# Earlier key and value loads with own buffers in a fused attention and mixture-of-experts kernel

## The chip, the cores and the metric

The kernel runs on one core of a Trainium2 chip. The metric is the device time of one execution in microseconds (us); the time before is the median of three runs.

## The reference

Three layers follow one another, all in float32: attention with a bias that a small network makes of relative positions, a token and channel mixer, and a mixture of experts in which each token goes to one expert. The change is in the attention:

```
B, H, S, D = q.shape                      # 2, 8, 576, 64
scores = np.matmul(q, k.transpose(0, 1, 3, 2)) / np.sqrt(D)
x = (log1p(abs(i - j)) / log1p(maximum(i, 1)))[..., None]
bias = np.maximum(x @ w1 + b1, 0.0) @ w2  # S x S x H, the same for both batches
attn = softmax(scores + bias.transpose(2, 0, 1))
out = np.matmul(attn, v)
```

## The kernel before

The order of all work is written out by hand. After a start section the attention runs in 40 steps. A step `s` stands for one tile of query rows, one batch and one pair of heads. The first tile holds the last 64 rows of the sequence for one pair (`it == NIT`); its eight steps, 0 to 7, take batch 0 in steps 0 to 3 and batch 1 in steps 4 to 7, two heads each. Then come four tiles of 128 rows with eight steps each, so step 8 is the first of tile 0. The mixers and the experts follow.

Keys: `load_k(i)` (L210) fetches the keys of four heads from HBM with five transfers, four of 128 KB (L216) and one of 64 KB (L217), in pieces of 256 bytes, into a buffer `kn`. There are two such buffers in turn: `load_k(0)` and `load_k(4)` share one, `load_k(2)` and `load_k(6)` the other. `key_T` (L251) transposes the keys on TensorE, ScalarE copies them into tiles `K` (L193), and `key_split` (L272) makes their low parts on VectorE. `key_T` and `key_split` of pair `s + 2` stand in step `s`.

Values: `load_v(b)` (L221) fetches all values of a batch with ten transfers, eight of 128 KB (L230) and two of 64 KB (L231), after two memsets on GpSimd (L228). `values` (L416) reads them first in step 2 for batch 0 and in step 6 for batch 1.

Bias: for each group of 16 rows `bias_hidden` (L478) makes the hidden layer on VectorE, ScalarE and GpSimd (L490, L487), `bias_mm` (L492) multiplies it with the second weights into PSUM, ScalarE copies that out into `ev` (L503), and a transfer brings `ev` into its rows of the bias tile: two transfers of 144 KB for each group of the last tile (L509, tile `bias4`), one of 288 KB for each group of the other tiles (L511). There are two `ev` buffers. The four groups of the last tile and the first of tile 0 stand in the start section, the other seven of tile 0 in steps 0 to 6. `softmax_tile` (L336) adds scores and bias and takes the maximum on VectorE (L337, a custom operation with output `t`) and the exponential on ScalarE (L340). It needs the whole bias tile: step 0 waits for all groups of `bias4`, step 8 for all eight of tile 0.

Queries: `load_q` (L234) loads queries into two buffers `qn`. The call in step 4 (L245) takes a buffer that `tail_split` of step 5 (L294, on GpSimd: L193 and L295 with output `qm`) must have read. Tiles from step 8 on have their split queries moved by four transfers of 128 KB each (L328, `qt<-qs`).

All these transfers are issued on one queue, that of SyncE (SP), in the order of the code: a transfer that has to wait holds all behind it. Eight semaphores serve them in turn, and an issue waits until the transfer eight places before it has landed. The order of the start section stands in the list `ORDER["start"]` (L58), the later loads in the loop over the steps (L659 to L662):

```
if s == 1:
    load_k(6)
if s == 2:
    load_v(1)
```

Of the kernel before, what the change touches and what calls it, by code (L numbers as in the profile page):

```python
# [9 lines left out]
F32 = mybir.dt.float32  # L10
# [11 lines left out]
B, H, S, D = 2, 8, 576, 64  # L22
# [32 lines left out]
QO = 3, 3, 3, 6  # L55

ORDER = {
    "start": "hidden0 const load_k2 tail_split0 hidden1 bias0 hidden2 bias1 key_T00 hidden3 zero key_T01 key_T11 key_T10 key_split0 tail_split1 bias2 hidden4 bias3 load_k4 hidden5 key_split1 tail_T bias4 load_v load_q".split(),  # L58
    "first": "scores0 hidden2 last_T prob_T0 values key_T0 normalize query_T tail_T query_split hidden1 hidden0 key_T1 bias_mm key_split out_T tail_split hidden3 query_rest".split(),
    "mixed": "hidden2 scores0 values tail_T query_T normalize hidden0 last_T prob_T0 key_T0 key_T1 query_split tail_split hidden1 key_split query_rest bias_mm out_T hidden3".split(),  # L60
    "bias": "query_T query_split hidden3 scores0 scores1 last_T values hidden0 query_rest hidden2 late bias_mm out_T mix prob_T0 prob_T1 hidden1 normalize".split(),
# [37 lines left out]
def body(ctx, tc, q, k, v, w1, b1, w2, wt1, wt2, wc1, wc2, wg, wl, mw1, mw2,  # L99
# [17 lines left out]
    with tc.manual_schedule():  # L117
        tok = ctx.enter_context(ExitStack())
        mix = TokenMix(nc, x)
        attention(tc, nc, tok, mix, q, k, v, w1, b1, w2, c_L, c_id, ident, x, wt1, wt2, prefill)  # L120
        if "x" in dbg:
            nc.sync.dma_start(dbg["x"], x)
        R = Routing(tc, nc, wg, wl, ident, c_tok, c_small, x2d, meta)
        X = Experts(tc, nc, R, Rings(tc, ctx, "big", side="right"), x_p, mw1, mw2, ident, x2d, meta, out)
        mixer(tc, nc, tok, mix, wc1, wc2, ident, x, R, X)
        if "x2" in dbg:
            nc.sync.dma_start(dbg["x2"], x2d)
        X.rest()
        X.close()
        R.close()  # L130


def attention(tc, nc, tok, mix, q, k, v, w1, b1, w2, c_L, c_id, ident, x, wt1, wt2, prefill):
# [9 lines left out]
    tw_p = pool(tok, "tokw")  # L143
    with ExitStack() as ctx:
        cst = pool(ctx, "acst")
        bias_p = pool(ctx, "bias", 2)
        nat_p = pool(ctx, "nat")
# [15 lines left out]
        def load_const():  # L163
            four = lambda ap, n: ap.rearrange("(a k) o -> a k o", a=1).to_broadcast([4, HID, n])

            cut = 4 * NG + S + 128
            warm = cst.tile([128, 1], F32, name="warm")
            nc.vector.memset(warm, 0.0)
            nc.scalar.activation(warm, warm, AF.Exp)
            nc.sync.dma_start(tabs[:, 0:cut], c_L[:, 0:cut])  # L170
            nc.scalar.dma_start(w1c, four(w1.rearrange("o k -> k o"), 1))
            nc.sync.dma_start(b1c, four(b1.rearrange("(k o) -> k o", o=1), 1))
            nc.sync.dma_start(w2r, four(w2, H))
            load_k(0)
            load_q(*steps[0])
            nc.sync.dma_start(tabs[:, cut:], c_L[:, cut:])
            nc.sync.dma_start(ident, c_id)

            zero = x[:, 0]
            nc.vector.memset(zero, 0.0)  # L180
            ps = alloc_ps()
            for _ in range(WARM):
                nc.tensor.matmul(ps, lhsT=zero[:, 0:128], rhs=zero, start=True, stop=True)
            nc.gpsimd.memset(wblk, 0.0)
            for ii in range(4):
                r = slice(32 * ii, 32 * ii + 32)
                nc.gpsimd.tensor_copy(wblk[r, 8 * ii:8 * ii + 8], w2r[r])
# [18 lines left out]


        nat = {}

        def load_k(i):  # L210

            b, pr = divmod(i, NP)
            n = nat_p.tile([128, 20, D], F32, name="kn", tag="kn", bufs=2)
            main, hs = n[:, 0:16].rearrange("p (n h) d -> p n h d", h=4), k[b, 2 * pr:2 * pr + 4]
            for j in range(NIT):
                nc.sync.dma_start(main[:, j], hs[:, 128 * j:128 * j + 128].rearrange("h p d -> p h d"))  # L216
            nc.sync.dma_start(n[0:64, 16:20], hs[:, 512:S].rearrange("h p d -> p h d"))  # L217
            for j in range(2):
                nat["k", i + j] = main[:, :, 2 * j:2 * j + 2], n[0:64, 16 + 2 * j:18 + 2 * j]

        def load_v(b):  # L221
            n = kv_p.tile([128, NIT + 1, H, D], F32, name=f"v{b}")


            nv, src = n.rearrange("p n (a e) d -> e p n a d", e=2), v[b].rearrange("(a e) p d -> e p a d", e=2)
            for e in range(2):
                r, z = (slice(64 * o, 64 * o + 64) for o in (e, 1 - e))
                nc.gpsimd.memset(nv[e][z, NIT], 0.0)  # L228
                for j in range(NIT):
                    nc.sync.dma_start(nv[e][:, j], src[e][64 * e + 128 * j:64 * e + 128 * j + 128])  # L230
                nc.sync.dma_start(nv[e][r, NIT], src[e][0:64] if e else src[e][512:S])  # L231
            nat["v", b] = n

        def load_q(it, i):  # L234

            b, pr = divmod(i, NP)
            n = nat_p.tile([128, 4, D], F32, name="qn", tag="qn", bufs=2)
            if it == NIT:
                tv = q[b, :, 512:S].rearrange("(a e) p d -> e p a d", e=2)
                for e in range(2):  # L240
                    nc.sync.dma_start(n[64 * e:64 * e + 64], tv[e])
                for j in range(NP):
                    nat["q", it, i + j] = n[:, j]
            else:
                nc.sync.dma_start(n, q[b, 2 * pr:2 * pr + 4, 128 * it:128 * it + 128].rearrange("h p d -> p h d"))  # L245
                nat["q", it, i] = n
# [271 lines left out]
        def fetch(p):  # L518
            n = p[1]
            if p[0] == 0:  # L520
                src = wt1[128 * n:min(128 * n + 128, S)]
            else:
                src = wt2[128 * n:128 * n + 128, HALF * p[2]:HALF * p[2] + HALF]
            raws[p] = fetch_f64(nc, nat_p, src, "kn", 2, p[0] == 0 and n == 4)
# [83 lines left out]
        def late_fetch(s):  # L608

            if pieces and any(f is decode for f, *_ in late.get(s, ())):  # L610
                fetch(pieces.pop(0))

        load_const()
        bias_setup()
        start = {
            "const": (bias_const,), "zero": (query_zero,), "load_k2": (load_k, 2), "load_k4": (load_k, 4), "load_v": (load_v, 0),
            "load_q": (load_q, *steps[NP]), "tail_T": (tail_T, *steps[0]),
        }
        for n in range(2):
# [11 lines left out]
        for s in range(N + 2):  # L631

            bias = gi < len(groups) and s < N and s >= B * NP * (its.index(groups[gi] // 8) - 1)
            at = lambda d, n=N: steps[s + d] if 0 <= s + d < n else None
            two = lambda d: (s + d) % 2 == 0 and s + d >= B * NP and at(d)
            hide = groups[gi + 1] if bias and gi + 1 < len(groups) else None
            todo = {
                "late": (late_step, (s,)), "mix": (mixes[s][0], mixes[s][1:]) if s in mixes else (None, None),
                "tail_split": (tail_split, at(2, B * NP)), "tail_T": (tail_T, at(1, B * NP)),
                "query_T": (query_T, two(QO[0])), "query_split": (query_split, two(QO[1])), "query_rest": (query_rest, two(QO[2])),  # L640
                "key_split": (key_split, at(2, B * NP)),
                "normalize": (normalize, at(0)), "last_T": (last_T, at(-1)),
                "values": (values, at(-2)), "out_T": (out_T, at(-2)),
                "bias_mm": (bias_mm, (groups[gi],) if bias else None),
            }
            for j in range(4):
                todo[f"hidden{j}"] = bias_hidden, hide is not None and (hide, (j,))
                todo[f"key_T{j}"] = key_T, j < 2 and at(2, B * NP) and (*at(2), j)
                todo[f"scores{j}"] = scores, at(0) and (*at(0), j)
                todo[f"prob_T{j}"] = prob_T, at(-1) and (*at(-1), j)  # L650
            if two(QO[3]):
                load_q(*steps[s + QO[3]])
            for name in ORDER["edge" if bias and s % (B * NP) == B * NP - 1 else "first" if s < 3 else "mixed" if s < B * NP else "bias" if bias else "plain"]:
                f, a = todo[name]
                if a:
                    f(*(a[1:] if f in (key_split, key_T) else a))
            gi += bias
            late_fetch(s - 1)
            if s == 1:  # L659
                load_k(6)  # L660
            if s == 2:
                load_v(1)  # L662
            if s == 10:
                prefill()
            if s == 8:
                for _ in range(2):
                    fetch(pieces.pop(0))
# [1095 lines left out]
```

## Time and profile before

| what | us |
|---|---|
| runs before | 583.7, 582.85, 583.69; median 583.69 |
| profiled execution | 584.03 |
| its span (first to last instruction) | 582.3 |
| PE busy in the span | 545.5 (94%) |
| DVE busy in the span | 383.9 (66%) |

The profiled execution takes 1.7 us more than its span, and 0.34 us more than the median. All times below are us from the start of the span. Engines: PE is TensorE, PEld its weight loads, DVE VectorE, ACT ScalarE, POOL GpSimd, SP SyncE; SPq is SyncE issuing a transfer, a name with `<-` is output and input of an instruction. An issue's duration is not that of the transfer. A wait in square brackets is the idle time of that engine just before the instruction, with what ended it.

### The profile page before, as it was taken

How to read it: one execution, taken by the hardware profiler on the slowest of the kernel's cores; microseconds unless marked ns; L12 is line 12 of the kernel's file. 1: busy time of each engine (PE TensorE's matmuls, PEld its weight loads, DVE VectorE, ACT ScalarE, POOL GpSimd, SP SyncE). 2: the span in 40 equal slices, each digit the busy share in tenths (PEclk: the TensorE clock that was granted, in tenths of full speed). 3: DMA queues.
4: the chain of work that ended last, by engine and by line, in shares of the span. 5: the costliest groups of instructions: out<-in, count | busy, mean ns of one | idle time of the engine just before them, and what ended most of it. 6: DMA issues, size and time to landing. Idle time of an engine off the chain costs nothing.

```text
span 582.3 us, 11959 instructions
## 1 busy us (share of the span) xinstructions
PE 545.5 (94%) x4306; PEld 430.3 (74%) x4306; DVE 383.9 (66%) x896; ACT 329.5 (57%) x608; POOL 242.1 (42%) x230
## 2 busy tenths in 40 slices
PE   7689699999899999989999999999999999999992
PEld 3366477777677887869999877787778778787871
DVE  5789588889887675698888535714473235668650
ACT  4678589789898793344444223221423257777760
POOL 4666547476555360044444300310014234657541
PEclk8979889999999999999999999999999999999997
DMA  6997988698697351143443020081002985566950
GB/s 162 130 173 126 142 158 165 132 177 157 127 147 126 77 154 38 37 138 120 148 161 126 1 91 0 1 302 61 19 18 43 370 299 175 147 230 245 367 185 12
DMA packets 72110, 79.90 MB, mean 137 GB/s; under 512 B 36822, under 2 KB 51420, under 8 KB 72044
## 3 DMA queue, kind: packets, MB, share of 16 engines
q1 hardware_dynamic: 67276, 73.72, 50.7%
q0 software_dynamic: 2176, 5.26, 2.7%
q8 instruction: 36, 0.59, 0.5%
q10 hardware_dynamic: 2592, 0.09, 0.3%
q14 instruction: 30, 0.25, 0.2%
HBM read 72.08 MB, written 5.34 MB: 133 GB/s over the span
## 4 chain that ended last, share of the span: by engine, by line
PE 65%; DVE 12%; DMA 7%; issue 5%; ACT 5%; SPq 2%; POOL 2%; ACTq 0%; POOLq 0%; DVEq 0%
PE ph L748 20%; PE po L748 16%; DMA bias<-ev 6%; PE py L748 5%; PE ps L500 5%; PE tp L425 4%; PE ps L359 3%; PE tp L410 3%; DVE t L337 2%; ACT t L340 2%; PE tp L748 1%; DVE K L272 1%; DMA mt<-meta 1%; PE tp L1448 1%; DVE raw L732 1%
## 5 line engine op out<-in xcount | busy, mean ns | idle before, releaser
L490 POOL TENSOR_SCALAR hd<-tabs,sc,negb 128x576 f32<-128x576 f32 x32 | 76.4, 2389 | 4.7 <-PE ps L500 3.0
L340 ACT ACTIVATE t<-t,st 128x576 f32<-128x576 f32 x72 | 55.4, 770 | 28.8 <-DVE st L337 28.4
L748 PE MATMUL po<-cw,h 128*128 128x512 f32 x272 | 67.3, 395 | 0.0
L337 DVE CUSTOM_DVE_ANT_0 t<-ps,bias 128x576 f32<-128x576 f32 x72 | 52.3, 751 | 16.1 <-DMA bias<-ev 6.6
L359 PE MATMUL ps<-K,qt 128*128 128x288 f32 x320 | 54.0, 309 | 4.4 <-DVE qt L199 3.5
L748 PEld LDWEIGHTS po<-cw,h 128*128 128x128 f32 x272 | 49.8, 188 | 10.0 <-issue 0.4
L1411 DVE TENSOR_TENSOR big<-raw,big 128x1024 fp32r<-128x1024 f32 x30 | 42.3, 1433 | 22.4 <-ACT big L1410 22.4
L500 PE MATMUL ps<-hd,wblk 128*32 128x288 f32 x576 | 47.7, 440 | 7.5 <-DVE st L337 6.5
L359 PEld LDWEIGHTS ps<-K,qt 128*128 128x128 f32 x320 | 45.0, 192 | 6.7 <-DVE qt L199 2.3
L425 PE MATMUL tp<-pt,v 128*64 128x128 f32 (+1 forms) x800 | 49.2, 268 | 0.6 <-DVE K L272 0.6
L748 PE MATMUL py<-big,hT 128*128 128x512 f32 x184 | 47.8, 400 | 0.4 <-POOL big L1411 0.4
L1189 POOL DMA_INDIRECT meta<-tokid,posi x10 | 10.0, 996 | 90.7 <-DVE tokid L1186 54.7
L425 PEld LDWEIGHTS tp<-pt,v 128*64 128x64 f32 x800 | 40.1, 137 | 8.1 <-issue 5.1
L1410 ACT CAST big<-raw 128x1024 fp32r<-128x1024 f32 x44 | 44.2, 1055 | 2.8 <-DMA big<-in_moe_w_dram 1.0
L748 PE MATMUL ph<-big,xT 128*128 128x512 f32 x168 | 42.9, 403 | 0.0
L490 DVE TENSOR_SCALAR hd<-tabs,sc,negb 128x576 f32<-128x576 f32 x69 | 42.2, 640 | 1.0 <-PE ps L500 0.9
L748 PEld LDWEIGHTS py<-big,hT 128*128 128x128 f32 x184 | 33.8, 188 | 8.6 <-POOL big L1411 0.9
L740 POOL TENSOR_TENSOR big<-wf,big 128x512 fp32r<-128x512 f32 x12 | 18.8, 1564 | 50.3 <-ACT big L739 50.3
L487 ACT ACTIVATE hd<-tabs,b1c,sc 128x576 f32<-128x576 f32 x43 | 36.9, 866 | 3.8 <-DVE sc L458 3.7
L1411 POOL TENSOR_TENSOR big<-raw,big 128x1024 fp32r<-128x1024 f32 x10 | 27.5, 2747 | 24.9 <-ACT big L1410 24.3
L748 PEld LDWEIGHTS ph<-big,xT 128*128 128x128 f32 x168 | 30.6, 189 | 8.6 <-issue 1.6
L500 PEld LDWEIGHTS ps<-hd,wblk 128*32 128x32 f32 x576 | 17.2, 115 | 24.1 <-DVE st L337 7.9
(302 smaller groups left out, 1204.7 us busy)
## 6 DMA issues: line engine op xcount, KB each, us to landing
raw<-in_moe_w_dram SPq DMA_DIRECT2D x48, 512.0 KB
raw<-in_moe_w_ch_dram SPq DMA_DIRECT2D x24, 512.0 KB
bias<-ev SPq DMA_DIRECT2D x32, 288.0 KB
qt<-qs SPq DMA_DIRECT2D x64, 128.0 KB
lw<-in_moe_w_dram SPq DMA_DIRECT2D x16, 512.0 KB
big<-in_moe_w_dram SPq DMA_DIRECT2D x8, 512.0 KB
lw<-in_moe_w_dram SPq DMA_DIRECT2D x16, 256.0 KB
big<-in_moe_w_dram SPq DMA_DIRECT2D x16, 256.0 KB
```

Of the source, the lines that this page charges most:

```text
L337: nc.vector.tensor_tensor_reduce(t.rearrange("p (a j) -> p a j", a=2), ps[:, :, 0:HALF], bs.rearrange("p (a j) -> p a j", a=2), op0=ALU.ad ...
L340: nc.scalar.activation(t, t, AF.Exp, bias=st[:, j:j + 1], scale=-1.0, accum_out=st[:, 2 + j:3 + j])
L359: nc.tensor.matmul(ps[:, hf, 0:HALF], lhsT=qt[:, j], rhs=K[k][:, hf * HALF:(hf + 1) * HALF], start=j == pairs[0][0], stop=j == pairs[-1][0])
L410: nc.tensor.transpose(tp[:, 128 * j:128 * j + 128], tt[:, o:o + 128], ident)
L425: nc.tensor.matmul(po[64 * h:64 * h + 64, 0:rhs.shape[1]], lhsT=lhsT, rhs=rhs, start=j == 0, stop=j == 4)
L487: nc.scalar.activation(hd[:, qq], Lt[:, o:o + S], AF.Relu, bias=b1c, scale=sc[:, c])
L490: eng.tensor_scalar(hd[:, qq], Lt[:, o:o + S], sc[:, c], negb, ALU.mult, ALU.max)
L500: nc.tensor.matmul(ps[32 * qq:32 * qq + 32, hf, 0:HALF], lhsT=wblk, rhs=hd[:, qq, hf * HALF:(hf + 1) * HALF], start=True, stop=True)
L740: nc.gpsimd.tensor_tensor(lo, src, hi.bitcast(F32), ALU.subtract)
L748: nc.tensor.matmul(out, lhsT=lhs[a], rhs=rhs[b], start=first and i == 0, stop=last and i == 2)
L1410: nc.scalar.copy(hi, raw)
L1411: (nc.gpsimd if c == 3 and t else nc.vector).tensor_tensor(lo, raw, hi.bitcast(F32), ALU.subtract)
```

## The change

The keys of batch 1 (`load_k(4)` and `load_k(6)`) get a tile of their own with two halves, `kn2`. It lies in the memory of `w2s`, which is first written in step 9. So these loads no longer wait for the readers of the first batch's keys. The issue order changes: `load_k(4)` goes ahead of the third group's bias transfers, `load_v(0)` ahead of the fourth group's, `load_k(6)` from step 1 to the start section, and `load_v(1)` from step 2 to step 0.

```
-    "start": "hidden0 const load_k2 tail_split0 hidden1 bias0 hidden2 bias1 key_T00 hidden3 zero key_T01 key_T11 key_T10 key_split0 tail_split1 bias2 hidden4 bias3 load_k4 hidden5 key_split1 tail_T bias4 load_v load_q".split(),
+    "start": "hidden0 const load_k2 tail_split0 hidden1 bias0 hidden2 bias1 load_k4 key_T00 hidden3 zero key_T01 key_T11 key_T10 key_split0 tail_split1 bias2 load_v hidden4 bias3 load_k6 hidden5 key_split1 tail_T bias4 load_q".split(),
...
         nat = {}
+        later = tw_p.tile([128, 2, 20, D], F32, name="kn2", tag="w2s")
...
-            n = nat_p.tile([128, 20, D], F32, name="kn", tag="kn", bufs=2)
+            n = later[:, i // 2 - 2] if b else nat_p.tile([128, 20, D], F32, name="kn", tag="kn", bufs=2)
...
-            if s == 1:
-                load_k(6)
-            if s == 2:
+            if s == 0:
                 load_v(1)
```

On VectorE, ScalarE and TensorE no instruction changes its place; on GpSimd the two memsets of each `load_v` move up with it. What moves stands on SP's queue.

First place: SP in the start section, from the last load of `load_k(2)` to the first group of tile 0. `bias_185` and `bias_186` are the bias of the last tile (`bias4`), `bias_310` and `bias_328` that of tile 0; `v_323` and `v_278` are the values of batch 0, `kn_104` is the new tile. Before:

```order
L216 DMA kn<-in_k_dram 128x4x64 x4
L217 DMA kn<-in_k_dram 64x4x64
L509 DMA bias_185<-ev 16x4x576 x8
L216 DMA kn<-in_k_dram 128x4x64 x4
L217 DMA kn<-in_k_dram 64x4x64
L511 DMA bias_310<-ev 16x8x576
L230 DMA v_323<-in_v_dram 128x4x64 x4
L231 DMA v_323<-in_v_dram 64x4x64
L230 DMA v_323<-in_v_dram 128x4x64 x4
L231 DMA v_323<-in_v_dram 64x4x64
```

With the change:

```order
L510 DMA bias_186<-ev 16x4x576 x4
L217 DMA kn_104<-in_k_dram 128x4x64 x4
L218 DMA kn_104<-in_k_dram 64x4x64
L510 DMA bias_186<-ev 16x4x576 x2
L231 DMA v_278<-in_v_dram 128x4x64 x4
L232 DMA v_278<-in_v_dram 64x4x64
L231 DMA v_278<-in_v_dram 128x4x64 x4
L232 DMA v_278<-in_v_dram 64x4x64
L510 DMA bias_186<-ev 16x4x576 x2
L217 DMA kn_104<-in_k_dram 128x4x64 x4
L218 DMA kn_104<-in_k_dram 64x4x64
L512 DMA bias_328<-ev 16x8x576
```

The eight transfers of `bias4` stood together; now five key loads stand behind the fourth and ten value loads behind the sixth, and the last two come behind those.

Second place: SP in steps 1 to 5. `v_574` and `v_404` are the values of batch 1, `qt_104` and `qt_105` the first query tile of step 8 on. Before, from the loads of `load_k(6)` on:

```order
L216 DMA kn<-in_k_dram 128x4x64 x4
L217 DMA kn<-in_k_dram 64x4x64
L245 DMA qn<-in_q_dram 128x4x64
L511 DMA bias_310<-ev 16x8x576
L230 DMA v_574<-in_v_dram 128x4x64 x4
L231 DMA v_574<-in_v_dram 64x4x64
L230 DMA v_574<-in_v_dram 128x4x64 x4
L231 DMA v_574<-in_v_dram 64x4x64
L511 DMA bias_310<-ev 16x8x576
L245 DMA qn<-in_q_dram 128x4x64
L511 DMA bias_310<-ev 16x8x576
L328 DMA qt_104<-qs 64x2x256 x4
```

With the change, from step 1's bias transfer on:

```order
L512 DMA bias_328<-ev 16x8x576
L246 DMA qn<-in_q_dram 128x4x64
L512 DMA bias_328<-ev 16x8x576 x2
L246 DMA qn<-in_q_dram 128x4x64
L512 DMA bias_328<-ev 16x8x576
L329 DMA qt_105<-qs 64x2x256 x4
```

The key and value loads are gone from between the bias transfers; from step 4's `load_q` on (the second `qn` row of each) the order is the same in both.

## Rows read from the trace of the kernel before

**Rows 1.** Stretches: length, busy us per engine (instructions), PEclk, DMA share, GB/s
```profile
16.00:18.00 2.00, 1.25 (x8) 0.34 (x6) 1.94 (x5) 1.14 (x2) 1.42 (x1) 1.00 0.15 25
18.00:20.00 2.00, 1.85 (x14) 0.52 (x12) 1.97 (x5) 1.53 (x3) 1.94 (x2) 1.00 0.57 139
...
28.00:34.00 6.00, 4.94 (x34) 2.94 (x33) 5.23 (x16) 4.66 (x9) 4.34 (x9) 0.52 1.16 183
40.00:60.00 20.00, 17.71 (x226) 12.83 (x225) 18.42 (x56) 16.62 (x30) 14.59 (x23) 1.00 0.86 133
...
72.00:582.00 510.00, 489.43 (x3723) 394.25 (x3723) 331.89 (x747) 282.82 (x528) 197.99 (x160) 0.99 0.49 136
```

**Rows 2.** Timeline of DVE: the bias-and-scores operation of steps 0 to 8
```profile
24.44 0.76 DVE L337 CUSTOM_DVE_ANT_0 t<-ps,bias 128x576 f32<-128x576 f32 x1 [2.96 <-PE tp L262]
30.07 0.76 DVE L337 CUSTOM_DVE_ANT_0 t<-ps,bias 128x576 f32<-128x576 f32 x1
36.08 0.76 DVE L337 CUSTOM_DVE_ANT_0 t<-ps,bias 128x576 f32<-128x576 f32 x1 [0.42 <-PE ps L359]
42.16 0.76 DVE L337 CUSTOM_DVE_ANT_0 t<-ps,bias 128x576 f32<-128x576 f32 x1
47.76 0.76 DVE L337 CUSTOM_DVE_ANT_0 t<-ps,bias 128x576 f32<-128x576 f32 x1
53.35 0.76 DVE L337 CUSTOM_DVE_ANT_0 t<-ps,bias 128x576 f32<-128x576 f32 x1
...
71.73 0.76 DVE L337 CUSTOM_DVE_ANT_0 t<-ps,bias 128x576 f32<-128x576 f32 x1 [4.87 <-DMA bias<-ev]
```

**Rows 3.** Chain of waits of the start section, in order of time: start, us, what
```profile
13.46 4.91 DMA bias<-ev
18.47 0.75 ACT ev L503
19.23 0.55 SPq L509
...
21.48 2.81 issue
24.44 0.76 DVE t L337
```

**Rows 4.** Timeline of ACT and PE around step 0
```profile
22.18 0.74 ACT L503 ACTIVATE ev<-ps,cb 128x576 f32<-128x576 f32 x1 [0.39 <-DMA bias<-ev]
23.56 0.27 PE L262 MATMUL tp<-ident,kn 64*128 64x64 f32 x1
```

**Rows 5.** DMA view of the stretch 24 to 34: rate in 40 slices, and total
```profile
GB/s 223 211 226 207 225 215 232 294 213 212 101 92 111 111 66 78 97 97 105 106 156 215 207 206 230 220 228 219 206 178 229 123 149 214 213 251 210 164 222 151
DMA packets 6209, 1.80 MB, mean 180 GB/s; under 512 B 6080, under 2 KB 6080, under 8 KB 6208
```

**Rows 6.** Waits for DMAs, whole span: waiter <- releaser: us in total, times, longest
```profile
DVE t L337 <- DMA bias<-ev: 6.6, 2, 4.9
...
ACT ev L503 <- DMA bias<-ev: 2.9, 4, 1.2
POOL qm L193 <- DMA qn<-in_q_dram: 1.8, 1, 1.8
...
PE ps L359 <- DMA qt<-qs: 1.0, 1, 1.0
```

**Rows 7.** Timeline of SP's queue: issues in steps 1 to 6
```profile
45.24 2.66 SPq L231 DMA_DIRECT2D v<-in_v_dram  x1
47.94 3.63 SPq L230 DMA_DIRECT2D v<-in_v_dram  x4
51.62 0.65 SPq L231 DMA_DIRECT2D v<-in_v_dram  x1
52.38 0.60 SPq L511 DMA_DIRECT2D bias<-ev  x1
57.17 0.38 SPq L245 DMA_DIRECT2D qn<-in_q_dram  x1
57.65 1.66 SPq L511 DMA_DIRECT2D bias<-ev  x1
...
64.14 0.58 SPq L511 DMA_DIRECT2D bias<-ev  x1
```

**Rows 8.** ACT's copies that step 3's and step 6's bias transfers read
```profile
46.34 0.74 ACT L503 ACTIVATE ev<-ps,cb 128x576 f32<-128x576 f32 x1
...
63.37 0.74 ACT L503 ACTIVATE ev<-ps,cb 128x576 f32<-128x576 f32 x1 [1.18 <-DMA bias<-ev]
```

**Rows 9.** Waits of SP's queue, 20 to 60
```profile
SPq L245 <- POOL qm L295: 3.7, 1, 3.7
...
SPq L216 <- PE tp L387: 0.6, 1, 0.6
```

**Rows 10.** Timeline of POOL in the start section: fifth hidden group, memsets of batch 0's values
```profile
16.58 3.18 POOL L490 TENSOR_SCALAR hd<-tabs,sc,negb 128x576 f32<-128x576 f32 x1 [1.41 <-PE ps L500]
...
19.83 0.67 POOL L228 MEMSET v<- 64x256 f32 x2
```

More of the change, by code (lines that the diff above doesn't have):

```diff
@@ L615, in attention @@
         start = {
-            "const": (bias_const,), "zero": (query_zero,), "load_k2": (load_k, 2), "load_k4": (load_k, 4), "load_v": (load_v, 0),
+            "const": (bias_const,), "zero": (query_zero,), "load_k2": (load_k, 2), "load_k4": (load_k, 4), "load_k6": (load_k, 6), "load_v": (load_v, 0),
             "load_q": (load_q, *steps[NP]), "tail_T": (tail_T, *steps[0]),
```

## The prediction

> **What bounds the kernel now.** I read the stretches first, then the softmax of the early steps, then what it waited for, then the queue. From 72 us to the end TensorE is busy 489.43 of 510 us [rows 1]: there only a later start of step 8 counts. Before that the steps are paced by VectorE, busy 18.42 of 20 us between 40 and 60 [rows 1]. The softmax operations of steps 0 to 5 start at 24.44, 30.07, 36.08, 42.16, 47.76 and 53.35, so a step takes 5.6 to 6.1 us; step 8 starts at 71.73 [rows 2]. Two places wait for a transfer of the bias. Step 8 stood 4.87 us on it [rows 2]. Step 0 at 24.44 shows 2.96 us of idle put down to a TensorE operation, but that one, L262, started at 23.56 and took 0.27 us, so it was over 0.6 us before [rows 2, 4]. What came last must be `bias4`: the chain goes through the ScalarE copy of its last group at 18.47 and the issue at 19.23 to the softmax at 24.44 [rows 3]. The list of waits for DMAs has twelve rows in the whole span; four stand here, and none of the twelve names a load of keys or values [rows 6]. So the loads that the change hurries are waited for by nobody.
>
> **The change part by part.**
>
> *Own buffers for batch 1's keys.* They take away the wait of `load_k` for readers: 0.6 us in all on the queue [rows 9]. Nobody waits for these keys [rows 6], so I cost it at nothing. The shared memory is written again in step 9, after the last reader in step 5: nothing.
>
> *Memsets on GpSimd.* The two for batch 0's values take 0.67 us and now stand ahead of the fifth hidden group's piece, before which GpSimd idled 1.41 us [rows 10]. Hidden: nothing. The two for batch 1 go from step 2 to step 0, off the chain.
>
> *Fifteen loads ahead of the last bias rows of step 0.* This is the term that counts. Before, the eight `bias4` transfers stood together. Now five key loads (4 x 128 + 64 = 576 KB) and ten value loads (8 x 128 + 2 x 64 = 1152 KB) stand between them, ahead of the last pair: 1728 KB or 1.77 MB. The softmax of step 0 needs that pair, and VectorE takes its work in order, so all of step 0 behind it stands too.
>
> How long do they hold the pair? In the stretch 24 to 34 the 0.25 us slices fall in two kinds: around 100 GB/s, which I read as the 288 KB bias transfer, and mostly 206 to 230 for the loads; the mean is 180 [rows 5]. I take 210: 1.77 / 0.210 = 8.4 us. From that goes what fits into an idle queue. ScalarE's copies show when pairs landed, as they wait for them: the second by 18.47, the third by 22.18 [rows 3, 4]. The last landed by 24.44, so a pair takes 2.26 us, and 22.18 - 18.47 - 2.26 = 1.45 us of queue stood empty between the second and the third. The key loads fill it. **Delay of step 0: 8.4 - 1.45 = 7.0 us**, to 31.4.
>
> Bounds: at the fast slices' 230 GB/s the loads take 7.7 us, and if all the idle share of the DMA engines from 16 to 20 were used, 2 x 0.85 + 2 x 0.43 = 2.56 us [rows 1], the delay is 5.1. At the mean of 180 they take 9.8, and less 1.45 the delay is 8.4.
>
> *What comes back in steps 0 to 8.* The queue is freer later: `load_k(6)` and batch 1's values no longer stand between the bias transfers of tile 0. Step 3's copy, from 46.34 to 47.08, was issued only at 52.38, behind value loads whose issues stretch to 2.66 and 3.63 us [rows 7, 8]. That wait of 5 us goes. But the next issue, `load_q` at 57.17, stands 3.7 us for GpSimd's `qm` of step 5 [rows 7, 9], and step 4's bias transfer, at 57.65, right behind it. This order is unchanged, so from step 5 on the end of tile 0's bias is tied to the steps and not to the loads: the transfer of 57.65 is awaited by ScalarE at 63.37, the last is issued at 64.14 and awaited by step 8 at 71.73 [rows 2, 7, 8]. Between the softmax of step 5 and that of step 8 lie 71.73 - 53.35 = 18.4 us as before. Worth: nothing.
>
> *The steps between.* Steps 1 and 2 took 6.01 and 6.08 us against 5.59 for step 4 [rows 2]. If fewer loads beside them make them as short, 0.91 us comes back. On the other side the granted clock was 0.52 between 28 and 34 [rows 1], a mix of 1.2 and 2.4 GHz, after TensorE had stood for step 0; standing 7 us longer could keep it low for two more steps, at 6.01 - 5.59 = 0.42 each, so 0.84. I take neither, since the dip should move along with step 0; both stay for the range.
>
> **Sum.** 584.03 (the profiled execution) + 7.0 = 591.0; on the median, 0.34 lower, **590.7 us**. Low end 583.7 + 5.1 - 0.9 = 587.9, high end 583.7 + 8.4 + 0.9 = 593.0.
>
> **Rivals.**
>
> *Nothing moves.* The loads fit beside the bias transfers, and step 0 starts within 1.2 us of now: 583.7 to 584.9. For it: a DMA share of 0.15 from 16 to 18 [rows 1]. Against it: 2.56 us of idle does not hold 7.7 us of loads, and a bias transfer behind other traffic takes long, 7.6 us from 64.14 to 71.73 [rows 2, 7]. The Trainium skill speaks for this rival in "DMA: Bandwidth & Descriptors", section "Rules for kernel authors": issue a DMA early and wait for it late, so that its fixed cost overlaps with compute. By that rule the time would be 583.7, since the loads were hidden already. The same page, section "Queues, rings and completion order", says that completion is not first-in-first-out per issuing engine, by which the bias pair could pass the loads; no row here shows a transfer that did. Chance 0.05.
>
> *Faster.* Step 8 is the place: if the bias of tile 0 is paced by the queue's total work and not by the steps, filling the idle 2.56 us between 16 and 20 [rows 1] ends that bias as much sooner, and step 8, which now stands 4.87 us [rows 2], takes up the late step 0: 583.7 - 2.6 = 581.1. It decides where the last bias transfer would be issued before 64.14 although step 5 is late. Against it: the queue stood empty before 57.17, for GpSimd [rows 7, 9]. Chance 0.05.
>
> *A part comes back.* Step 0 is 7 us late, but part of step 8's 4.87 us absorbs it, by up to 4.87: 585.8 to 587.9. The earlier issue in step 3 speaks for it, the tie to step 5 against it. Chance 0.12.
>
> *More is lost.* The later loads (`load_k(6)`, batch 1's values) also hold bias transfers that a ScalarE copy awaits, since there are two `ev` buffers; a second stop of the size of the 1.18 us before 63.37 [rows 8] on top of the high end gives 594 or more. Chance 0.05.
>
> **How the numbers follow.** My forecast, 587.9 to 593.0 with 590.7 as its value, has 0.73. 0.2%, about what a measurement of this kernel can tell, is 1.2 us. Slower: 0.73 + 0.12 + 0.05 = 0.90; same 0.05; faster 0.05. The range reaches down into the partial case to 586.5 and up to 593.0; it leaves out 0.05 + 0.05 + 0.05 and about 0.04 of the partial case, 0.19 in all.
>
> **What would show it.** Right: step 0's softmax starts near 31.4, between 29.5 and 32.8, with VectorE idle some 10 us before it; the steps after it keep 5.6 to 6.1 us; from step 5 to step 8 it is again some 18.4 us with a wait for the bias of some 5 us; from step 8 on everything is shifted by one amount. Step 3's bias transfer is issued within 1 us of its copy. Wrong: step 0 before 29 (the loads are passed or are faster than 230 GB/s), or fewer than 17 us from step 5 to step 8 (the end of the bias was paced by the queue).

## The result and the profile after

| | median us | runs | against the kernel before |
|---|---|---|---|
| before | 582.84 | 582.45 to 583.70, 6 runs | |
| changed | 591.21 | 589.40 to 593.77, 6 runs | 1.0136, 95% interval 1.0111 to 1.0161 |

The change makes the kernel slower by 1.4%; the forecast was 590.7. That forecast stood on a median of 583.69 from three runs of the kernel before; over six it is 582.84, so the medians lie 8.4 us apart where 7.0 were forecast. The profiled execution of the changed kernel takes 591.89 us, its span is 590.1 against 582.3.

The timeline of VectorE shows where. The names are those of [rows 2], the lines one higher (L338 for L337), for steps 0 to 5 and 8 to 10:

```profile
32.00 0.76 DVE L338 CUSTOM_DVE_ANT_0 t<-ps,bias 128x576 f32<-128x576 f32 x1 [11.75 <-DMA bias<-ev]
37.62 0.76 DVE L338 CUSTOM_DVE_ANT_0 t<-ps,bias 128x576 f32<-128x576 f32 x1
43.25 0.76 DVE L338 CUSTOM_DVE_ANT_0 t<-ps,bias 128x576 f32<-128x576 f32 x1
49.19 0.76 DVE L338 CUSTOM_DVE_ANT_0 t<-ps,bias 128x576 f32<-128x576 f32 x1
54.78 0.76 DVE L338 CUSTOM_DVE_ANT_0 t<-ps,bias 128x576 f32<-128x576 f32 x1
60.37 0.76 DVE L338 CUSTOM_DVE_ANT_0 t<-ps,bias 128x576 f32<-128x576 f32 x1
...
78.43 0.76 DVE L338 CUSTOM_DVE_ANT_0 t<-ps,bias 128x576 f32<-128x576 f32 x1 [4.83 <-DMA bias<-ev]
...
84.26 0.76 DVE L338 CUSTOM_DVE_ANT_0 t<-ps,bias 128x576 f32<-128x576 f32 x1 [1.66 <-PE ps L360]
...
89.22 0.76 DVE L338 CUSTOM_DVE_ANT_0 t<-ps,bias 128x576 f32<-128x576 f32 x1
```

Step 0 starts at 32.00 instead of 24.44, 7.56 us later, and the profile now names what VectorE stood for during 11.75 us: a bias transfer. Step 5 starts at 60.37, 7.02 later, and step 8 at 78.43, 6.70 later, with nearly the same wait as before, 4.83 against 4.87 us [rows 2]. Step 10 starts 89.22 - 81.38 = 7.84 us later, and so does the end: 590.1 - 582.3 = 7.8. All of the loss is there by step 10, 6.70 us of it by step 8. Step 10 in the timeline of before:

```profile
81.38 0.76 DVE L337 CUSTOM_DVE_ANT_0 t<-ps,bias 128x576 f32<-128x576 f32 x1
```

The queue of SP shows what stands in front of step 0:

```profile
14.08 2.80 SPq L217 DMA_DIRECT2D kn<-in_k_dram  x4
16.92 1.52 SPq L218 DMA_DIRECT2D kn<-in_k_dram  x1
18.55 1.20 SPq L510 DMA_DIRECT2D bias<-ev  x2
19.79 2.31 SPq L231 DMA_DIRECT2D v<-in_v_dram  x4
22.14 1.49 SPq L232 DMA_DIRECT2D v<-in_v_dram  x1
23.67 2.26 SPq L231 DMA_DIRECT2D v<-in_v_dram  x4
25.98 0.65 SPq L232 DMA_DIRECT2D v<-in_v_dram  x1
26.72 1.24 SPq L510 DMA_DIRECT2D bias<-ev  x2
...
64.19 0.38 SPq L246 DMA_DIRECT2D qn<-in_q_dram  x1
65.11 0.96 SPq L512 DMA_DIRECT2D bias<-ev  x1
```

The same pair in the kernel before:

```profile
19.23 1.18 SPq L509 DMA_DIRECT2D bias<-ev  x2
```

The last pair of `bias4` is issued at 26.72, 7.49 us later than before; step 0's softmax starts 32.00 - 27.96 = 4.0 us after the end of that issue, as long as before (20.41 to 24.44). The lower rows of the first view are the unchanged place: step 4's query load and its bias transfer, held for GpSimd of step 5.

The stretches show the engines idle meanwhile (columns as in [rows 1]):

```profile
24.00:29.00 5.00, 3.10 (x21) 1.03 (x19) 0.00 (x0) 0.74 (x1) 0.00 (x0) 0.69 1.29 214
...
28.00:34.00 6.00, 0.00 (x0) 0.00 (x0) 1.03 (x5) 1.20 (x3) 0.00 (x0) 0.71 1.25 182
47.00:67.00 20.00, 17.85 (x226) 12.97 (x225) 18.42 (x56) 16.78 (x30) 13.80 (x21) 1.00 0.32 51
...
79.00:590.00 511.00, 490.49 (x3723) 395.18 (x3723) 332.21 (x747) 283.05 (x528) 198.62 (x160) 0.99 0.49 135
```

From 24 to 29, where mostly value loads move, the rate is 214 GB/s. From 28 to 34 TensorE does nothing. Between 47 and 67, the old stretch 40 to 60 moved by 7, VectorE is busy the same 18.42 of 20 us although the DMA share fell from 0.86 to 0.32 [rows 1]: the loads had left the stretch, and it did not get shorter. After step 8 the busy times are those of before.

### The profile page after: what moved, and what is told of

The parts are those of the page before. It is cut to its first block, busy times and chain, and to the rows that moved or that the text cites. A ratio compares the mean times of both kernels' runs of the same rounds, so it can differ in the third digit from the quotient of the medians.

```text
span 590.1 us, 11952 instructions
## 1 busy us (share of the span) xinstructions
PE 548.5 (93%) x4306; PEld 432.9 (73%) x4306; DVE 384.0 (65%) x896; ACT 329.7 (56%) x608; POOL 242.0 (41%) x230
## 4 chain that ended last, share of the span: by engine, by line
PE 64%; DVE 12%; DMA 7%; ACT 5%; issue 5%; SPq 2%; POOL 2%; ACTq 0%; POOLq 0%; DVEq 0%
PE ph L747 19%; PE po L747 15%; DMA bias<-ev 5%; PE py L747 5%; PE ps L501 5%; PE tp L426 4%; PE ps L360 3%; PE tp L411 3%; DVE t L338 2%; ACT t L341 2%; DVE K L273 2%; PE tp L747 1%; DVE hd L491 1%; PE tp L1447 1%; DMA mt<-meta 1%
## 5 line engine op out<-in xcount | busy, mean ns | idle before, releaser
L338 DVE CUSTOM_DVE_ANT_0 t<-ps,bias 128x576 f32<-128x576 f32 x72 | 52.3, 751 | 25.2 <-DMA bias<-ev 19.7
L360 PE MATMUL ps<-K,qt 128*128 128x288 f32 x320 | 56.9, 320 | 9.9 <-DVE qt L199 8.8
L360 PEld LDWEIGHTS ps<-K,qt 128*128 128x128 f32 x320 | 47.2, 200 | 12.5 <-DVE qt L199 8.2
L501 PE MATMUL ps<-hd,wblk 128*32 128x288 f32 x576 | 45.8, 431 | 8.8 <-DVE st L338 6.5
L504 ACT ACTIVATE ev<-ps,cb 128x576 f32<-128x576 f32 x36 | 26.6, 739 | 15.6 <-PE ps L501 7.5
```

Source lines behind the costliest of these rows:

```text
L338: nc.vector.tensor_tensor_reduce(t.rearrange("p (a j) -> p a j", a=2), ps[:, :, 0:HALF], bs.rearrange("p (a j) -> p a j", a=2), op0=ALU.ad ...
L360: nc.tensor.matmul(ps[:, hf, 0:HALF], lhsT=qt[:, j], rhs=K[k][:, hf * HALF:(hf + 1) * HALF], start=j == pairs[0][0], stop=j == pairs[-1][0])
L501: nc.tensor.matmul(ps[32 * qq:32 * qq + 32, hf, 0:HALF], lhsT=wblk, rhs=hd[:, qq, hf * HALF:(hf + 1) * HALF], start=True, stop=True)
L504: nc.scalar.activation(ev.rearrange("p (a b) -> p a b", a=2), ps[:, :, 0:HALF], AF.Identity, bias=cbs[hidden_by(g).replace("P", "V")])
```

## The experiments

The theory is the forecast's: the loads ahead of the last `bias4` pair hold step 0, by their bytes; the rest of the change costs and gives nothing. The rivals: the new tile, or the loads moved into steps 0 and 1, cost the time; or the bytes on full DMA engines cost it, wherever they stand in the queue. All ratios are against the kernel before on the same chip.

**The values of batch 0 put back** (the changed kernel, batch 0's values behind the first group of tile 0 again):

```
-... bias2 load_v hidden4 bias3 load_k6 hidden5 key_split1 tail_T bias4 load_q
+... bias2 hidden4 bias3 load_k6 hidden5 key_split1 tail_T bias4 load_v load_q
```

> The changed kernel with one part undone: the values of batch 0 are loaded behind the first group of tile 0 again, as before; keys stay early and in their own tile. Theory (loads ahead of the last bias4 pair hold step 0, by their bytes over some 210 GB/s less 1.45 us of empty queue): only the 576 KB of keys are ahead of it, 2.8 us, so step 0's softmax starts at 25.5 to 26.5 instead of 32.0, and the time is 1 to 2.5 us above the kernel before (584 to 585.5). Rival (the later loads or the new tile cost the time): step 0 may start early, but the time stays near 590.

```profile
26.90 0.76 DVE L338 CUSTOM_DVE_ANT_0 t<-ps,bias 128x576 f32<-128x576 f32 x1 [6.77 <-DMA bias<-ev]
```

SP's timeline of this run has the last pair here:

```profile
20.38 1.18 SPq L510 DMA_DIRECT2D bias<-ev  x2
```

Step 0 (VectorE's row above) starts at 26.90, 5.1 us before the changed kernel's, and 2.46 after the kernel before. The ratio is 1.0051 (1.0029 to 1.0073), about 3.0 us, with a median of 586.17. The direction is that of the theory, but 576 KB of keys cost 2.46 us and not the 1.1 to 2.1 forecast; the measured time is above the 585.5 given. The pair is issued only 1.15 us later than before (20.38 against 19.23), so the larger part of the 2.46 us passes after its issue.

**The values alone** (the kernel before, batch 0's values ahead of the fourth group):

```
-... bias2 hidden4 bias3 load_k4 hidden5 key_split1 tail_T bias4 load_v load_q
+... bias2 load_v hidden4 bias3 load_k4 hidden5 key_split1 tail_T bias4 load_q
```

> The kernel before with one part of the change alone: the values of batch 0 are loaded ahead of the fourth bias4 group; keys as before. Theory: 1152 KB are ahead of the last pair, 5.6 us, with little empty queue left to fill, so step 0 starts at 29.5 to 30.5 and the time is 5 to 6.5 us above the kernel before (588 to 589.5). Rival (it takes keys and values together, or the new tile): below 586.

```profile
30.14 0.76 DVE L337 CUSTOM_DVE_ANT_0 t<-ps,bias 128x576 f32<-128x576 f32 x1 [9.68 <-DMA bias<-ev]
```

Step 0 starts at 30.14, 5.70 us late, within what was expected. Ratio 1.0122 (1.0105 to 1.0139), median 589.65, a little above the 589.5 given. 1152 KB, or 1.18 MB, in 5.70 us are 207 GB/s, the rate that the forecast took as 210. The new tile is not in this kernel, and the batch 1 loads are where they were: most of the loss needs neither.

That the bytes set these 5.70 us is not shown. SP's timeline has the first four loads and the pair behind all ten:

```profile
18.95 2.30 SPq L230 DMA_DIRECT2D v<-in_v_dram  x4
...
25.04 1.24 SPq L509 DMA_DIRECT2D bias<-ev  x2
```

SP's list of waits names no transfer in this stretch, so the 25.04 - 18.95 = 6.1 us are ten issues one after another, and the pair goes out 25.04 - 19.23 = 5.81 us later than before. Here the time of issuing ten loads is a rival to their bytes, of the same size; with the keys alone the issue explains less than half. No run has the same bytes in fewer transfers, which would tell the two apart.

**The new tile alone** (the kernel before with the two lines of the change that make and use `kn2`, all loads in their old places):

> The kernel before with the new tile for batch 1's keys alone; all loads stay in their old places. Theory (order costs the time, the tile nothing): step 0 at 24.4 to 24.7, time within 0.8 us of the kernel before. Rival (the tile's place in memory or its waits cost): 2 us or more above.

VectorE's timeline of this run, steps 0 and 5:

```profile
24.81 0.76 DVE L338 CUSTOM_DVE_ANT_0 t<-ps,bias 128x576 f32<-128x576 f32 x1 [4.49 <-PE tp L263]
...
53.16 0.76 DVE L338 CUSTOM_DVE_ANT_0 t<-ps,bias 128x576 f32<-128x576 f32 x1
```

Ratio 0.9996 (0.9980 to 1.0012), median 583.67; step 0 at 24.81, a little over the 24.7 given. The tile costs and gives nothing that can be told.

**The last pair on another queue** (the changed kernel; the two transfers of the fourth group are issued by ScalarE):

```
-                    nc.sync.dma_start(bv[:, 0], ev[e::2])
+                    (nc.scalar if g == NG - 1 else nc.sync).dma_start(bv[:, 0], ev[e::2])
```

> The changed kernel with the last bias4 pair issued on ScalarE's queue instead of SP's; the bytes and the loads stay. Theory (place in the queue, not bytes): the pair no longer stands behind ten value loads, step 0 starts at 24.5 to 27 and the time is 583 to 586. Rival (the DMA engines are full, so the bytes decide whatever the queue): step 0 still starts at 29 or later, time above 588.

ScalarE's timeline, with its own issue of the pair, and VectorE's of step 0:

```profile
19.82 1.33 ACTq L510 DMA_DIRECT2D bias<-ev  x2
...
50.70 0.74 ACT L504 ACTIVATE ev<-ps,cb 128x576 f32<-128x576 f32 x1 [1.98 <-DMA bias<-ev]
```

```profile
27.35 0.76 DVE L338 CUSTOM_DVE_ANT_0 t<-ps,bias 128x576 f32<-128x576 f32 x1 [6.92 <-DMA bias<-ev]
```

The pair goes out at 19.82 and step 0 starts at 27.35, 4.65 us before the changed kernel's, with the same bytes under way. So the place in the queue makes the larger part of the 7.56 us. The rest is neither theory's: after the end of the issue the pair needs 27.35 - 21.15 = 6.2 us where it needs 4.0 on SP's queue. SP's loads move at the same time; that they slow the pair is likely and was not tested by itself. The key loads also still stand ahead of the third pair, and alone they cost 2.46. The median, 587.44 (ratio 1.0068, 1.0045 to 1.0091), lies between the two theories' numbers and outside both. Part of it is a stop at another place, the 1.98 us of the second row: step 3's copy waits for a transfer two places back.

**All moved loads behind the last pair** (the changed kernel; keys 4, values 0 and keys 6 behind the fourth group):

```
-... hidden2 bias1 load_k4 key_T00 ... tail_split1 bias2 load_v hidden4 bias3 load_k6 hidden5 ...
+... hidden2 bias1 key_T00 ... tail_split1 bias2 hidden4 bias3 load_k4 load_v load_k6 hidden5 ...
```

> The changed kernel with the new tile and all batch 1 loads kept early, but every moved load of the start section (keys 4, values 0, keys 6) issued behind the last bias4 transfer. Theory: no load is ahead of a bias4 transfer, step 0 starts at 24.4 to 24.7 as before, and the time is within 1 us of the kernel before (582.3 to 584), with no gain either, since nobody waited for these loads. Rival (the tile, or the loads of step 0 and 1 between tile 0's bias transfers, cost the time): over 586.

This was wrong in the total: median 588.43, ratio 1.0091 (1.0073 to 1.0108), which is the number that the rival gave; the next run shows that the rival's cause is not the one. VectorE's timeline of steps 0, 2 and 3, and ScalarE's copies into `ev`:

```profile
24.69 0.76 DVE L338 CUSTOM_DVE_ANT_0 t<-ps,bias 128x576 f32<-128x576 f32 x1 [4.18 <-PE tp L263]
...
35.92 0.76 DVE L338 CUSTOM_DVE_ANT_0 t<-ps,bias 128x576 f32<-128x576 f32 x1
46.97 0.76 DVE L338 CUSTOM_DVE_ANT_0 t<-ps,bias 128x576 f32<-128x576 f32 x1 [1.05 <-PE ps L360]
```

```profile
28.34 0.74 ACT L504 ACTIVATE ev<-ps,cb 128x576 f32<-128x576 f32 x1
39.45 0.74 ACT L504 ACTIVATE ev<-ps,cb 128x576 f32<-128x576 f32 x1 [5.20 <-DMA bias<-ev]
```

Step 0 is back at 24.69, as the theory says, but step 3 follows step 2 by 11.05 us. The loss has moved: the first bias transfer of tile 0 now stands behind twenty loads, and step 1's copy, which needs the `ev` buffer that this transfer reads, waits 5.20 us for it. VectorE waits for ScalarE, which is stopped in that copy. That is the forecast's rival "more is lost", in another kernel than it was named for.

**The same with three `ev` buffers:**

```
-            ev = nat_p.tile([128, S], F32, name="ev", bufs=2)
+            ev = nat_p.tile([128, S], F32, name="ev", bufs=3)
```

> The run with all moved loads behind the last bias4 transfer, now with three ev buffers instead of two. That run lost 5.2 us where step 1's copy waited for the first transfer of tile 0, which stands behind 25 loads. Theory (two buffers make a copy wait for a transfer two places back): with a third the copy of step 1 waits for nothing, step 3's softmax follows step 2's by 5.6 to 6.1 us instead of 11, and the time is 582 to 585. Rival (the transfer's late landing itself holds the steps, or the longer queue shows elsewhere): time 587 or more.

```profile
23.23 0.76 DVE L338 CUSTOM_DVE_ANT_0 t<-ps,bias 128x576 f32<-128x576 f32 x1 [3.03 <-PE tp L260]
...
34.47 0.76 DVE L338 CUSTOM_DVE_ANT_0 t<-ps,bias 128x576 f32<-128x576 f32 x1
40.40 0.76 DVE L338 CUSTOM_DVE_ANT_0 t<-ps,bias 128x576 f32<-128x576 f32 x1
```

Step 3 follows step 2 by 5.93 us (the first transfer of tile 0 stands behind 20 loads, not the 25 of the expectation). Median 582.63, ratio 0.9991 (0.9975 to 1.0007): no loss, with every early load kept, though behind the last pair, and no gain that can be told.

**Step 8's wait** (the kernel before; step 4's query load behind the step's work):

```
-            if two(QO[3]):
+            if two(QO[3]) and s != 4:
                 load_q(*steps[s + QO[3]])
...
             gi += bias
+            if s == 4:
+                load_q(*steps[s + QO[3]])
```

> The kernel before with one call moved: step 4's query load is issued behind that step's work, so the bias transfer of step 4 no longer stands behind its wait for GpSimd of step 5. Theory (step 8's wait of 4.87 us comes from that place in the queue, not from loads of keys and values): the transfer goes out right after its copy, at 52.7 to 53.5 instead of 57.65, steps 0 to 5 stay, step 8 starts 3 to 5 us earlier (66.7 to 68.7), time 579 to 581. Rival (the query transfers or the later bias transfers end last anyway): step 8 within 1 us of 71.7, time 582.5 to 584.

```profile
69.44 0.76 DVE L337 CUSTOM_DVE_ANT_0 t<-ps,bias 128x576 f32<-128x576 f32 x1 [3.71 <-POOL hd L490]
```

Step 8 starts at 69.44 instead of 71.73, and steps 0 to 5 stay. So the place in the queue did hold step 8, but only 2.3 us of the 4.87 go, where 3 to 5 were expected: the last bias transfer still comes late. It is now issued at 62.84 by SP's timeline, right behind its copy, and in the trace it lands at 69.22. Step 8 starts 0.2 us after that landing, as in the kernel before (71.51 and 71.73), so the wait is for the transfer, although the row names an instruction of GpSimd that ended at 69.44. Median 582.05, ratio 0.9971 (0.9953 to 0.9989), 1.7 us faster and above the 581 given.

**Late query load and three `ev` buffers, on the kernel before:**

> The kernel before with step 4's query load behind its step's work and three ev buffers. Theory: besides the gain of the late query load, the copies of the start section no longer wait 0.34 and 0.99 us for transfers, nor step 6's copy 1.18 us; step 0 starts 0.5 to 1.5 us earlier than 24.4, step 8 at 65 to 67.5, time 577.5 to 580. Rival (the queue, not the buffers, paces the start): same as with the late query load alone, within 0.5 us.

Its chain of waits has the last bias transfer, and VectorE's timeline step 8:

```profile
61.44 6.53 DMA bias<-ev
```

```profile
68.18 0.76 DVE L337 CUSTOM_DVE_ANT_0 t<-ps,bias 128x576 f32<-128x576 f32 x1 [3.91 <-POOL hd L490]
```

The row names GpSimd again, but the chain runs through the transfer, from 61.44 to 67.97. Step 0 at 23.55, step 8 at 68.18; median 581.67, ratio 0.9968 (0.9951 to 0.9985). Both steps start earlier, step 8 less so than expected, and the time lies above the 580 given. In the time, the third buffer adds nothing here that can be told from the run before.

**All three together** (loads behind the last pair, three `ev` buffers, late query load):

> All three together: the moved loads behind the last bias4 transfer, three ev buffers, and step 4's query load behind its step's work. Theory: what the change set out to do costs nothing once no bias transfer that is awaited stands behind a load, and the late query load shortens step 8's wait as it did alone; step 0 at 23.2 to 23.8, step 8 at 66.5 to 68.5, time 579.5 to 582. Rival (the earlier loads still take something back): not faster than 582.5.

```profile
23.41 0.76 DVE L338 CUSTOM_DVE_ANT_0 t<-ps,bias 128x576 f32<-128x576 f32 x1 [2.99 <-DMA bias<-ev]
...
68.69 0.76 DVE L338 CUSTOM_DVE_ANT_0 t<-ps,bias 128x576 f32<-128x576 f32 x1 [3.69 <-POOL hd L491]
```

Median 580.72, ratio 0.9938 (0.9914 to 0.9962): 0.6% below the kernel before, and the fastest of the study; step 8 at 68.69 is a little over the 68.5 given. Its interval overlaps that of the two runs before it, so that the early loads themselves bring something is not shown.

## Why the prediction was right

*The term that counts, the fifteen loads.* Forecast 7.0 us on step 0, measured 7.56, within the bounds of 5.1 and 8.4. That the loads hold the pair is shown by the runs with the values alone, with the pair on the other queue and with the loads behind it. The two halves of the term came out unlike. The rate of 210 GB/s agrees with the 207 for the values alone and with the 214 of the stretch 24 to 29, though issuing ten loads takes as long, so bytes over rate need not be the reason for the number. The credit for the empty queue, 1.45 us, was too large: keys alone should have cost 576 KB at 210 GB/s, 2.8, less 1.45, so 1.4, and cost 2.46. In the changed kernel 8.4 - 7.56 = 0.8 us of credit are left. The gap between the landings of two pairs was read as empty queue. But the third pair was issued at 17.50 by SP's timeline of before, and the stretch with a DMA share of 0.15 lies from 16 to 18 [rows 1]: the gap holds that pair's own time from issue to landing, and the idle stretch lies largely ahead of it; how much of the idle stretch the keys filled was not measured by itself.

*Own buffers and memsets at nothing.* Shown for the tile by the run with it alone; the memsets have no run of their own.

*Step 8's wait unchanged.* 60.37 to 78.43 are 18.06 us, against 18.4 forecast and 18.38 before, and the wait is 4.83 us. Step 3's bias transfer goes out right behind its copy now, at 54.13 by SP's timeline, and nothing that can be told came of that, as worked out. The run with the late query load shows that the tie lay in that one call, though moving it frees only about half of the wait.

*The steps between.* From step 0 to step 5 they took 60.37 - 32.00 = 28.37 us instead of 28.91: 0.54 of the 0.91 us that were kept for the range. It need not come from fewer loads beside them: the run with the tile alone has all loads in their old places and takes 53.16 - 24.81 = 28.35 us.

*One thing the forecast did not have.* It said that from step 8 on everything is shifted by one amount. The shift grows from 6.70 at step 8 to 7.84 at step 10. The stretches around step 8, of the changed kernel and then of the kernel before, show the granted clock, the third number from the right:

```profile
75.00:79.00 4.00, 0.00 (x0) 0.00 (x0) 0.57 (x1) 0.00 (x0) 2.31 (x2) 0.92 1.02 139
79.00:83.00 4.00, 3.75 (x25) 1.93 (x26) 3.46 (x12) 2.75 (x6) 0.00 (x0) 0.50 0.30 70
83.00:87.00 4.00, 4.00 (x46) 2.94 (x45) 2.61 (x8) 3.55 (x8) 2.69 (x2) 0.73 0.91 176
```

```profile
68.00:72.00 4.00, 0.24 (x10) 0.10 (x4) 0.27 (x1) 0.00 (x0) 2.58 (x2) 0.65 1.08 152
72.00:76.00 4.00, 3.45 (x23) 1.63 (x24) 3.76 (x12) 2.45 (x6) 0.00 (x0) 0.50 0.32 74
76.00:80.00 4.00, 4.00 (x54) 3.06 (x54) 2.93 (x9) 3.96 (x9) 2.52 (x2) 0.99 0.83 145
```

In both TensorE had stood before step 8 and works at 1.2 GHz after it. Before, the clock is back by 76, some 4 us into step 8; in the changed kernel 83 to 87 still shows 0.73, and step 9 waits 1.66 us for TensorE. That the clock makes the 1.1 us is read from these rows and was not tested. It need not be the change's. In the run with the late query load, which leaves all key and value loads in their old places, step 10 follows step 8 by 80.22 - 69.44 = 10.78 us, here by 10.79, before by 9.65; in the run with the tile alone it is 9.96. The row of step 10 with the late query load:

```profile
80.22 0.76 DVE L337 CUSTOM_DVE_ANT_0 t<-ps,bias 128x576 f32<-128x576 f32 x1
```

*How good the number is.* In the profiles 7.56 us at step 0, less 0.54 in the steps to 5 and 0.32 to step 8, plus 1.14 behind step 8, make 7.84. So the term that was forecast was 0.6 us too small, and three terms that the sum had at nothing nearly cancel. That 590.7 lies 0.5 us from the measured median is luck in part: the difference of the medians, 8.4 us (the interval of the ratio is 6.5 to 9.4), is 1.4 over the forecast 7.0, and the base of the forecast was 0.85 too high.

*The rivals.* "Nothing moves" fell: step 0 moved. So did, for this kernel, what the prediction drew from the rule of the Trainium skill ("DMA: Bandwidth & Descriptors", section "Rules for kernel authors") that a DMA issued early overlaps its fixed cost; in the run with three `ev` buffers, where no transfer that is awaited in time stands behind the loads, the early loads cost nothing that can be told, as the rule has it. No transfer passed another on SP's queue: between 12 and 36 us, in the traces of both kernels and of the runs with the values put back, with the values alone, with the pair on the other queue and with all loads behind it, its transfers land in the order of their issue. The pair came earlier only on the other queue. "Faster" and "a part comes back" fell with step 8's unchanged wait.

## What to carry to other kernels

An early load on a queue that works in order delays the transfers behind it, here five loads of 576 KB by 2.5 us and ten of 1152 KB by 5.7, whether or not anyone waits for the load; whether their bytes or their number set the amount is open. So first look for who waits for the load (here nobody, so there was nothing to win), then for who waits for the transfers that it is put in front of, including those that only free a buffer. A transfer that waits for another engine, as step 4's query load, deserves the last place among its neighbours in such a queue.

## What the runs showed that was not expected

A transfer pair moved to another queue did not become free of the loads: the step that awaits it started 6.2 us after its issue ended instead of 4.0. In the same run the four value loads on SP, 2.31 us of issuing in the changed kernel, took 6.47. The first row is SP's timeline, the second SP's list of waits from 15 to 30:

```profile
19.84 6.47 SPq L231 DMA_DIRECT2D v<-in_v_dram  x4
```

```profile
SPq L231 <- DMA bias<-ev: 3.7, 1, 3.7
```

So this is not slow issuing but a wait: the fourth load went out at 25.94, after 3.7 us for a bias transfer. In the trace it uses the same semaphore as the first transfer of the pair, which landed at 25.92. The semaphores that serve the transfers in turn serve both queues, so a transfer on ScalarE's queue can still hold one on SP's.

The changed kernel's six runs lie between 589.40 and 593.77, 4.4 us apart, where the six of the kernel before are 1.25 apart. That is no trait of the change: the 35 runs of the kernel before that stand beside the later experiments lie 4.35 apart (581.17 to 585.52), and the 13 beside the first ones 3.9. What makes runs of one kernel so different stays open.
